# The square of two feed-forward pairs in three goes to PSUM instead of SBUF beside stage two

## The chip, the core and the metric

The kernel runs on one core of one Trainium2 chip. The metric is device time in microseconds (us) of one execution. Five engines work side by side, each through its own queue in order: TensorE (PE, with its weight loads shown as PEld), VectorE (DVE), ScalarE (ACT), GpSimd (POOL) and SyncE (SP), which here only issues DMAs. TensorE writes PSUM, eight banks of 512 float32 columns by 128 partitions; the other data lie in SBUF.

## The reference

```python
u = x * v                                   # 4 x 12480 x 128
h_filt = (np.maximum(pos_emb @ w1, 0.0) @ w2) * window
Uf = np.fft.rfft(u, n=2 * S, axis=1)
Hf = np.fft.rfft(h_filt, n=2 * S, axis=0)
y = np.fft.irfft(Uf * Hf[None], n=2 * S, axis=1)[:, :S]
z = (x * y).reshape(49920, 128)
out = (np.maximum(z @ w_in, 0.0) ** 2) @ w_out   # 128 -> 2048 -> 128
```

A long convolution by FFT for four batches, and after it a feed-forward whose activation is the squared relu. All of it is float32.

## The kernel before

The convolution of a batch goes through four stages (`stage1` to `stage4`), each a generator that yields 1, 2, 3 in every step; `chain()` strings the stages of all batches together. The feed-forward is cut into 98 token tiles of up to 512 tokens (`NM`) and, in each, into 8 pairs of 128 hidden rows (`NS`): 784 pairs. The main loop runs pair after pair and lets the convolution of the next batches advance in between with `adv(1)`, `adv(2)`, `adv(3)`. The schedule is manual: each engine runs its instructions in the order in which the code writes them. When all of the convolution is done, the rest of the pairs runs alone.

To keep float32 accuracy each operand is split into a high and a low part, and each product takes three matmuls (`mm3`, L100 to L102: high x high, low x high or its mirror, high x low). One pair goes as follows.

- `m_h` (L786): six matmuls write the pair's hidden values into a two-bank PSUM tile `A`. The pool `psa` has two such tiles, so four of the eight banks. One bank is `O`, three are the tiles `F` of the convolution.
- `m_g` (L792): ScalarE writes `r` = relu(`A`) to SBUF (L800), and then `gh`, the rounded high part of `r` squared (L803). The exact square comes in one of three ways. Way "p": VectorE writes max(`A`, 0) times `r` back over `A` (L805). Way "t": ScalarE squares `r` in place (L807). Way "b" also squares `r` in place, and VectorE makes `gh` from it (L814).
- `m_l` (L810): VectorE subtracts, `gl` = square minus `gh` (L819).
- `m_o` (L824): six matmuls, two pairs later in the loop, add the pair into `O`; the third of the six is the first that reads `gl`.

`way(n)` (L860) picks the way: beside stage two of a batch every third pair is "p" and the other two are "t"; beside stage three "b"; beside the other stages "p"; after the convolution "b".

In a turn of the loop the order on TensorE is: `m_h` of pair n, `m_o` of pair n-2, then the convolution's matmuls. Beside stage two these are L386, which write an `F` bank. VectorE multiplies that by the filter's spectrum `ht` (L421, twice per step), ahead of the subtraction of the pair, and GpSimd combines the products (L423, L424). The spectrum is loaded by SyncE's queue one step ahead (`ht<-Hd`). While batch 1 is in the convolution, the loop also takes an extra stage-two step every few pairs (`EXTRA`); beside the stage two of batches 2 and 3 it does not. These three stretches of the run are called the first, second and third block below.

A tile of a pool can be given out again when the last instruction that uses it has run; the next `m_h` into it then waits for that instruction.

Of the kernel before, what the change touches and what calls it, by code (L numbers as in the profile page):

```python
# [11 lines left out]
AF = mybir.ActivationFunctionType  # L12
# [37 lines left out]
def hyena_moe_kernel(  # L50
# [19 lines left out]
    nc = tc.nc  # L70
# [721 lines left out]
    def m_g(A, p, n, between, way):  # L792

        r = p.tile([128, 2, GM], F32, tag="r", name="r")[:, :, :n]
        hi = p.tile([128, 2, GM], F32R, tag="gh", name="gh")[:, :, :n]
        h = A[:, :, :n]
        nc.scalar.activation(r, h, AF.Relu)  # L800
        between()
        if way != "b":
            nc.scalar.activation(hi, r, AF.Square)  # L803
        if way == "p":
            nc.vector.scalar_tensor_tensor(out=h, in0=h, scalar=0.0, in1=r, op0=ALU.max, op1=ALU.mult)  # L805
            return p, h, hi, way
        nc.scalar.activation(r, r, AF.Square)  # L807
        return p, r, hi, way

    def m_l(st, share):  # L810
        p, g, hi, way = st
# [60 lines left out]
    for i in range(NM):  # L872
        for f in range(NS):
            adv(1)
            A = m_h(zT, f)
            last = m_o(*pend.pop(0)) if len(pend) > 1 else None
            adv(2)
            if not nxt[0] and not tail:
                tail.append(ctx.enter_context(pool("tp")))
                tail[0].tile([128, TP], F32, name="shift", bufs=1)  # L880
            late.append((i, f, m_g(A, tail[0] if tail and f % 2 else mp, GN[i], lambda: m_out(last), way(i * NS + f))))
            while len(late) > len(tail):
                x, y, st = late.pop(0)
                pend.append((x, y, m_l(st, False)))
            if i + 1 < NM:
                if f == (1 if i else 3):
                    ready(i + 1)
                    zi = zload(i + 1)
                if f == (4 if i else 6):
                    nzT = zsplit(zi)  # L890
            adv(3)
            n = i * NS + f
            if stage[0] != since[0]:
                since = stage[0], n + 4
            owed += EXTRA[done[1] > 0]
            if owed >= 1 and stage[0] in (("s3", "s4") if done[1] else ("s2", "s3", "s4")) and nxt[0] == 1 and n >= since[1]:
                owed -= 1
                since = stage[0], n + 3
                for k in range(1, 4):
                    adv(k)  # L900
# [144 lines left out]
```

## Time and profile before

| | before |
|---|---|
| median of 3 runs | 3066.09 us (3065.58 to 3071.74) |
| the profiled execution | 3062.8 us |
| its span on the core | 3060.9 us |
| TensorE busy | 3021.9 us, 99% of the span |
| VectorE busy | 2510.9 us, 82% |
| ScalarE busy | 2389.7 us, 78% |
| GpSimd busy | 1469.1 us, 48% |
| granted TensorE clock | 0.999 |

The profile is one execution. Busy time is the time in which an engine runs an instruction; waits lie between. Matmuls are pipelined, so a matmul of 0.39 us may be followed by the next one 0.23 us later: for TensorE the starts tell more than the durations. "gl<-r,gh" reads: writes gl, reads r and gh. "<-DVE gl" behind a row names what ended the idle time ahead of it.

### The profile page before, as it was taken

To read this page: it belongs to the slowest core of one execution; us is meant where nothing else is said; L and a number is where in the kernel's file an instruction comes from. 1 tells how busy PE (TensorE), PEld (TensorE's weight loads), DVE (VectorE), ACT (ScalarE), POOL (GpSimd) and SP (SyncE) were. 2 spreads that over 40 slices of the span, in tenths; PEclk is the share of its full clock that TensorE was granted. 3 is DMA by queue.
4 is the path that set the end of the run, shared out by engine and by line. 5 is a ranking of instruction groups with operands and counts; after the bars stand their busy time and mean duration, and the time that the engine had idled before them with its cause. 6 is when DMAs were issued, how large, how long until landed. Compare 5 with 4: busy or idle time off the path is not lost.

```text
span 3060.9 us, 48765 instructions
## 1 busy us (share of the span) xinstructions
PE 3021.9 (99%) x16010; PEld 2557.2 (84%) x16010; DVE 2510.9 (82%) x3056; ACT 2389.7 (78%) x3110; POOL 1469.1 (48%) x1595
## 2 busy tenths in 40 slices
PE   9989999999999999999999999999999999999999
PEld 8768888878888888888888888888888888888887
DVE  7888888878878988878877898878877898777776
ACT  5557777777888787788888877788888877888887
POOL 1249665647544665556544665646544563000000
PEclk9999999999999999999999999999999999999999
DMA  5782665444101664334200575434300474000000
GB/s 181 275 291 75 158 170 139 120 116 148 44 22 47 166 169 124 117 109 125 80 15 27 139 179 145 131 93 120 104 22 15 111 177 109 25 24 26 24 26 20
DMA packets 288753, 322.00 MB, mean 105 GB/s; under 512 B 95716, under 2 KB 214484, under 8 KB 288500
## 3 DMA queue, kind: packets, MB, share of 16 engines
q1 hardware_dynamic: 259348, 268.40, 30.3%
q0 software_dynamic: 29152, 50.48, 6.3%
q8 instruction: 128, 2.10, 0.3%
q14 instruction: 125, 1.02, 0.1%
HBM read 230.35 MB, written 64.55 MB: 96 GB/s over the span
## 4 chain that ended last, share of the span: by engine, by line
PE 88%; DMA 3%; DVE 3%; POOL 2%; issue 2%; ACT 1%; SPq 1%; DVEq 0%; ACTq 0%; POOLq 0%
PE A L100 11%; PE A L101 11%; PE A L102 11%; PE O L102 8%; PE O L101 8%; PE O L100 8%; PE F L386 5%; PE F L498 5%; PE F L298 4%; PE F L100 4%; PE F L102 4%; PE F L101 4%; PE A L296 2%; POOL W L411 1%; DMA xt<-x 1%
## 5 line engine op out<-in xcount | busy, mean ns | idle before, releaser
L800 ACT ACTIVATE r<-A 128x1020 f32<-128x1020 f32 (+2 forms) x784 | 804.2, 1026 | 410.7 <-PE A L102 397.1
L819 DVE TENSOR_TENSOR gl<-r,gh 128x1020 fp32r<-128x1020 f32 (+1 forms) x434 | 637.3, 1468 | 105.1 <-ACT r L807 68.1
L100 PE MATMUL A<-zh,wt 128*128 128x510 f32 (+2 forms) x1568 | 667.3, 426 | 1.8 <-DVE gl L819 1.5
L101 PE MATMUL A<-zh,wt 128*128 128x510 f32 (+2 forms) x1568 | 610.2, 389 | 0.0
L102 PE MATMUL A<-zl,wt 128*128 128x510 f32 (+2 forms) x1568 | 609.9, 389 | 0.0
L803 ACT ACTIVATE gh<-r 128x1020 fp32r<-128x1020 f32 (+1 forms) x452 | 477.3, 1056 | 61.0 <-PE O L101 53.3
L102 PE MATMUL O<-gl,wt 128*128 128x510 f32 (+1 forms) x1216 | 475.8, 391 | 3.6 <-DVE gl L819 3.5
L805 DVE SCALAR_TENSOR_TENSOR A<-A,r 128x1020 f32<-128x1020 f32 (+1 forms) x349 | 424.3, 1216 | 64.9 <-ACT r L800 63.0
L819 DVE TENSOR_TENSOR gl<-A,gh 128x1020 fp32r<-128x1020 f32 (+1 forms) x349 | 425.2, 1218 | 63.5 <-ACT gh L803 20.3
L101 PE MATMUL O<-gh,wt 128*128 128x510 f32 (+1 forms) x1216 | 472.1, 388 | 0.0
L100 PE MATMUL O<-gh,wt 128*128 128x510 f32 (+1 forms) x1216 | 472.0, 388 | 0.0
L807 ACT ACTIVATE r<-r 128x1020 f32<-128x1020 f32 (+1 forms) x435 | 461.0, 1060 | 12.5
L814 DVE CAST gh<-r 128x1020 fp32r<-128x1020 f32 (+1 forms) x332 | 232.6, 701 | 211.7 <-ACT r L807 210.7
L783 POOL TENSOR_TENSOR zl<-zi,zh 128x510 fp32r<-128x510 f32 (+1 forms) x97 | 126.6, 1305 | 536.1 <-PE A L102 427.7
L571 POOL TENSOR_TENSOR al<-W,ah 104x512 fp32r<-104x512 f32 x214 | 282.2, 1319 | 187.8 <-ACT ah L565 185.8
L102 PEld LDWEIGHTS A<-zl,wt 128*128 128x128 f32 x1568 | 294.4, 188 | 63.1
L507 POOL TENSOR_TENSOR W<-c 104x224 f32<-104x224 f32 x256 | 215.5, 854 | 264.6 <-ACT c L505 261.5
L100 PEld LDWEIGHTS A<-zh,wt 128*128 128x128 f32 x1568 | 296.0, 189 | 51.2 <-DVE gl L819 4.7
L101 PEld LDWEIGHTS A<-zh,wt 128*128 128x128 f32 x1568 | 296.3, 189 | 42.7
L423 POOL TENSOR_TENSOR W<-W,m 112x256 f32<-112x256 f32 x156 | 167.9, 1076 | 229.0 <-DVE m L421 207.0
L102 PEld LDWEIGHTS O<-gl,wt 128*128 128x128 f32 x1216 | 228.0, 187 | 53.0 <-DVE gl L819 5.7
L101 PEld LDWEIGHTS O<-gh,wt 128*128 128x128 f32 x1216 | 227.8, 187 | 47.5
(126 smaller groups left out, 5413.2 us busy)
## 6 DMA issues: line engine op xcount, KB each, us to landing
ht<-Hd SPq DMA_DIRECT2D x208, 256.0 KB
tb<-t POOLq DMA_DIRECT2D x224, 208.0 KB, 3.5
xt<-x SPq DMA_DIRECT2D x224, 128.0 KB
xt<-xs SPq DMA_DIRECT2D x96, 224.0 KB
vt<-vs SPq DMA_DIRECT2D x96, 224.0 KB
zd<-zs SPq DMA_DIRECT2D x333, 64.0 KB
out<-ot SPq DMA_DIRECT2D x79, 255.0 KB
tb<-t2s SPq DMA_DIRECT2D x156, 112.0 KB
```

The costliest lines, as they stand in the source:

```text
L100: nc.tensor.matmul(o, lh, rh, start=first, stop=False)
L101: nc.tensor.matmul(o, ll, rh, start=False, stop=False)
L102: nc.tensor.matmul(o, lh, rl, start=False, stop=last)
L423: nc.gpsimd.tensor_sub(out=re[0], in0=re[0], in1=im[1])
L507: nc.gpsimd.tensor_sub(out=dst[:, 1], in0=c[:, :, 0:3:2], in1=c[:, :, 3:0:-2])
L571: eng.tensor_sub(out=lo, in0=w, in1=hi.bitcast(F32))
L800: nc.scalar.activation(r, h, AF.Relu)
L803: nc.scalar.activation(hi, r, AF.Square)
L805: nc.vector.scalar_tensor_tensor(out=h, in0=h, scalar=0.0, in1=r, op0=ALU.max, op1=ALU.mult)
L807: nc.scalar.activation(r, r, AF.Square)
L814: nc.vector.tensor_copy(hi, g)
L819: nc.vector.tensor_sub(out=lo, in0=g, in1=hi.bitcast(F32))
```

## The change

Where the way is "t", ScalarE's second square is written over the pair's PSUM tile `A` instead of over `r`. The subtraction of that pair (L819 before, L820 after, as all lines from there on move by one) then reads `A` and `gh` instead of `r` and `gh`. Ways "p" and "b" stay as they are.

```diff
@@ m_g
         if way == "p":
             nc.vector.scalar_tensor_tensor(out=h, in0=h, scalar=0.0, in1=r, op0=ALU.max, op1=ALU.mult)
             return p, h, hi, way
-        nc.scalar.activation(r, r, AF.Square)
-        return p, r, hi, way
+        g = h if way == "t" else r
+        nc.scalar.activation(g, r, AF.Square)
+        return p, g, hi, way
```

No engine's order changes; what changes is who waits for whom. On TensorE, at the start of the first block: the last matmuls of one pair's `m_o` and the first of the `m_h` of pair 6767 (a "t" pair, as is the pair 6713 that had the same PSUM tile). The number behind a name tells the tile apart.

```order
 L100 MATMUL O_6520<-gh_6707,wt_1568 128x510 [waits Activation_49]
 L101 MATMUL O_6520<-gh_6707,wt_1568 128x510
-L102 MATMUL O_6520<-gl_6711,wt_1568 128x510 [waits DVE_49]
+L102 MATMUL O_6520<-gl_6711,wt_1568 128x510
 L100 MATMUL O_6520<-gh_6707,wt_1568 128x510
 L101 MATMUL O_6520<-gh_6707,wt_1568 128x510
 L102 MATMUL O_6520<-gl_6711,wt_1568 128x510
-L100 MATMUL A_6767<-zh_6606,wt_1037 128x510 [waits Activation_49]
+L100 MATMUL A_6767<-zh_6606,wt_1037 128x510 [waits DVE_49]
 L101 MATMUL A_6767<-zh_6606,wt_1037 128x510
 L102 MATMUL A_6767<-zl_6607,wt_1037 128x510
```

The first matmul of `m_h` waited for ScalarE, which had read the tile with its relu; now it waits for VectorE, whose subtraction is the tile's last reader. The wait for VectorE at the third matmul of `m_o` is gone, since the earlier one covers it. In the built program before, the "t" pairs of a block all follow each other in one of the two tiles of `psa`, and the "p" pairs have the other to themselves, because a "t" tile comes free first; in the changed program the pairs alternate between the two, so each `m_h` waits for the subtraction of the pair two before it.

On ScalarE, the same pairs: relu, high part and square of two "t" pairs, and the start of a "p" pair.

```order
 L800 ACTIVATE r_6706<-A_6693 128x2x510 [waits DVE_49,PE_49]
 L803 ACTIVATE gh_6707<-r_6706 128x2x510 [waits DVE_49,PE_49,Activation_49]
-L807 ACTIVATE r_6706<-r_6706 128x2x510 [waits Activation_49]
+L808 ACTIVATE A_6693<-r_6706 128x2x510
 L800 ACTIVATE r_6726<-A_6713 128x2x510 [waits DVE_49,PE_49]
 L803 ACTIVATE gh_6727<-r_6726 128x2x510 [waits DVE_49,PE_49,Activation_49]
-L807 ACTIVATE r_6726<-r_6726 128x2x510 [waits Activation_49]
```

The square in place had to wait until the instruction that makes `gh` had read `r`; the square into `A` has no wait of its own.

## Rows read from the trace of the kernel before

**Rows 1.** The page: each engine's busy time; the chain that ended last.

```profile
PE 3021.9 (99%) x16010; PEld 2557.2 (84%) x16010; DVE 2510.9 (82%) x3056; ACT 2389.7 (78%) x3110; POOL 1469.1 (48%) x1595
...
PE 88%; DMA 3%; DVE 3%; POOL 2%; issue 2%; ACT 1%; SPq 1%; DVEq 0%; ACTq 0%; POOLq 0%
```

**Rows 2.** Busy us by stretch (PE, PEld, DVE, ACT, POOL): first two blocks.

```profile
635.00:787.00 152.00, 148.91 (x661) 121.10 (x659) 126.72 (x155) 110.03 (x111) 109.60 (x108) 1.00 0.48 139
1318.00:1503.00 185.00, 185.00 (x823) 151.90 (x822) 153.90 (x171) 149.06 (x151) 115.85 (x108) 1.00 0.42 121
```

**Rows 3.** The page, costliest groups: busy us, mean ns of one | idle before.

```profile
L807 ACT ACTIVATE r<-r 128x1020 f32<-128x1020 f32 (+1 forms) x435 | 461.0, 1060 | 12.5
L814 DVE CAST gh<-r 128x1020 fp32r<-128x1020 f32 (+1 forms) x332 | 232.6, 701 | 211.7 <-ACT r L807 210.7
```

**Rows 4.** Groups by shape, same columns: both subtractions, and a PSUM copy.

```profile
L819 DVE TENSOR_TENSOR gl<-r,gh 128x1020 fp32r<-128x1020 f32 x291 | 446.7, 1535 | 90.2 <-ACT r L807 68.1 <-PE A L102 1.9 <-PE F L498 0.5
L819 DVE TENSOR_TENSOR gl<-A,gh 128x1020 fp32r<-128x1020 f32 x341 | 416.5, 1221 | 62.5 <-ACT gh L803 20.3 <-ACT ah L565 1.0 <-PE A L102 0.6
...
L434 ACT COPY A<-F 112x256 f32<-112x256 f32 x52 | 18.1, 349 | 1.6
```

**Rows 5.** Timeline (start us, us, engine): VectorE and GpSimd around 2098.

```profile
2098.35 3.85 DVE L819 TENSOR_TENSOR gl<-r,gh 128x1020 fp32r<-128x1020 f32 x1 [0.42 <-ACT r L807]
...
2099.85 1.27 POOL L783 TENSOR_TENSOR zl<-zi,zh 128x510 fp32r<-128x510 f32 x1
```

**Rows 6.** Who waited for whom, first block: us in total, times, longest.

```profile
DVE W L421 <- DMA ht<-Hd: 13.2, 11, 3.7
...
PE O L102 <- DVE gl L819: 3.0, 2, 1.9
```

**Rows 7.** The same view, second block.

```profile
DVE W L421 <- DMA ht<-Hd: 5.1, 4, 1.8
```

**Rows 8.** The same view, third block.

```profile
DVE W L421 <- DMA ht<-Hd: 6.9, 7, 1.4
```

**Rows 9.** Timeline, first block: a late spectrum, its "p" pair, and TensorE.

```profile
698.41 0.69 DVE L421 TENSOR_TENSOR W<-F,ht 112x512 f32<-112x512 f32 x1 [1.15 <-DMA ht<-Hd]
...
702.16 1.22 DVE L819 TENSOR_TENSOR gl<-A,gh 128x1020 fp32r<-128x1020 f32 x1
702.17 0.59 PE L100 MATMUL A<-zh,wt 128*128 128x510 f32 x1
...
704.19 0.39 PE L102 MATMUL O<-gl,wt 128*128 128x510 f32 x1
```

**Rows 10.** Timeline, third block: a "p" pair with no late spectrum.

```profile
2069.74 1.22 DVE L819 TENSOR_TENSOR gl<-A,gh 128x1020 fp32r<-128x1020 f32 x1
...
2071.60 0.59 PE L100 MATMUL A<-zh,wt 128*128 128x510 f32 x1
```

**Rows 11.** Timeline: the first "t" pair of the first block.

```profile
622.74 1.22 DVE L819 TENSOR_TENSOR gl<-r,gh 128x1020 fp32r<-128x1020 f32 x1 [2.77 <-ACT r L807]
...
623.26 0.39 PE L100 MATMUL A<-zh,wt 128*128 128x510 f32 x1
```

**Rows 12.** Timeline: the end of the first block.

```profile
787.22 0.39 PE L100 MATMUL A<-zh,wt 128*128 128x510 f32 x1
...
787.34 1.27 DVE L819 TENSOR_TENSOR gl<-r,gh 128x1020 fp32r<-128x1020 f32 x1 [0.81 <-ACT r L807]
```

**Rows 13.** Timeline: the end of the third block.

```profile
2210.58 0.42 PE L100 MATMUL A<-zh,wt 128*128 128x510 f32 x1
...
2211.42 1.22 DVE L819 TENSOR_TENSOR gl<-A,gh 128x1020 fp32r<-128x1020 f32 x1
...
2212.70 0.50 PE L102 MATMUL O<-gl,wt 128*128 128x510 f32 x1
```

**Rows 14.** Timeline, ScalarE: a square and the instruction behind it.

```profile
2039.61 1.06 ACT L807 ACTIVATE r<-r 128x1020 f32<-128x1020 f32 x1
...
2040.57 0.60 ACT L782 CAST zh<-zi 128x510 fp32r<-128x510 f32 x1
```

## The prediction, made before the run

> **What bounds the kernel now.** I read the busy times and the chain that ended last first: TensorE is busy for 3021.9 of 3060.9 us and makes up 88% of the chain [rows 1]. The reader is to see that a gain on another engine is worth nothing here unless TensorE waited for it, while a wait put on TensorE is lost one for one. Next the stretches in which the change acts. In the second block TensorE is busy for 185.00 of 185.00 us, while VectorE has 153.90 and ScalarE 149.06; the first block has 148.91 of 152.00 [rows 2]; the third block's row reads as the second's. The clock was granted in full, 1.00, in both. Then the waits inside the blocks, and at last the timeline, to see how long before each `m_h` the subtraction of the pair two earlier had ended: that is the wait which the change adds.
>
> **The change part by part.** How many pairs: 435 squares in place, of which 332 belong to way "b" (each has a cast on VectorE), so 435 - 332 = 103 are of way "t" [rows 3]. They lie in the three blocks, some 34 in each.
>
> *The square itself.* The trace has no ScalarE write into PSUM of this size. Bounds: 0.70 us, what VectorE's cast of as many columns takes [rows 3], and 4 x 0.349 = 1.40 us, four copies of 256 columns into PSUM with their fixed part counted four times [rows 4]. I take 1.06 us, the square in place, the nearest row [rows 3]: no change. At 1.40 every "t" subtraction would come 0.34 us later, which ScalarE has room for, but which adds to the waits below. In place, the square waits for the instruction before it to end; an instruction without such a wait starts 2040.57 - 2039.61 = 0.96 us after a square of 1.06 us [rows 14]. So the "t" chain gets 0.1 us shorter.
>
> The trace has no two equal ScalarE instructions that differ in the destination alone. The Trainium skill, "ScalarE: Activation LUTs", section "Step-by-step: what each stage is for", calls PSUM the destination of lower latency for ScalarE, with the caveat that this is of use only if TensorE doesn't need most of PSUM. By the tip alone the sum would be a few tenths of a microsecond better; by its caveat it turns over, since this kernel's pools fill all eight banks. The rest of this part is what the caveat means here, from rows.
>
> *The subtraction.* Read from `r` it takes 1.535 us in the mean, read from `A` 1.221 us [rows 4]: 0.31 us x 103 = 32 us of VectorE's time go. They are not on TensorE's path: in the first block TensorE waited for `gl` twice, 3.0 us in all [rows 6], and in the second hardly at all [rows 2]. I cost them at nothing, except where they bring a subtraction forward (below).
>
> *The added wait.* Before, a "t" pair's tile was free after its relu. Now it is free after its subtraction, and `m_h` of pair n waits for that of pair n-2. The same subtraction was already needed by the third matmul of `m_o`, so it is needed earlier: by 704.19 - 702.17 = 2.02 us [rows 9]. "P" pairs had that tile to themselves and were late without harm: in rows 9 the subtraction ends at 702.16 + 1.22 = 703.38, while the `m_h` that will now wait for it started at 702.17. Queued behind the waiting `m_h` on TensorE are its other five matmuls, `m_o` of the pair two earlier and the convolution's L386; ScalarE's relu and VectorE's L421 wait for these. So TensorE's delay moves everything behind it. Where is `m_h` late, and how much?
>
> 1. First pairs of each block. No L386 is between them yet. The subtraction ends at 622.74 + 1.22 = 623.96, `m_h` started at 623.26 [rows 11]: 0.7 us late. Three blocks, and I add 0.4 us once for a second late pair in the first: 2.5 us.
> 2. Inside the first block. With the extra steps VectorE has two steps' L421 ahead of the "p" pair, so that pair has no time to spare, and what a late spectrum costs passes through. VectorE waited 13.2 us for spectra there, and 3.0 us of it already reached TensorE [rows 6]: 13.2 - 3.0 = 10.2 us. The example: a spectrum 1.15 us late gives an `m_h` that is 703.38 - 702.17 = 1.2 us late [rows 9].
> 3. Inside the other two. A "p" pair there has spare time: 2071.60 - (2069.74 + 1.22) = 0.64 us [rows 10]. VectorE waited 5.1 us in 4 waits [rows 7] and 6.9 us in 7 [rows 8]; less 0.64 us each, 12.0 - 11 x 0.64 = 5.0 us. A few fall on a "t" pair and cost less.
> 4. Ends of the blocks. The L421 of the last step and the change of way find TensorE without L386 to fill in. 787.34 + 1.27 - 787.22 = 1.4 us late in the first [rows 12], 2211.42 + 1.22 - 2210.58 = 2.1 us in the third, of which the third matmul of `m_o`, 2212.70 - 2210.58 = 2.12 us behind, has already waited for some 0.1 us more than the 2.02 us of rows 9 [rows 13]. With a follower that is late as well I take 2 us each: 6.0 us.
>
> Sum: 2.5 + 10.2 + 5.0 + 6.0 = 23.7 us. About 27 late places, each 0.1 us less late through the earlier square: -2.7 us. Net +21 us. Against the profiled execution, 3062.8 us, that is 3084 us; the median of the runs before is 3.3 us above it, so I predict 3087 us.
>
> The bounds of this sum: if a held TensorE gives the spectra time to arrive, terms 2 and 3 vanish and 2.5 + 6.0 - 0.6 = 8 us stay; if nothing is absorbed, the chain is not shortened and the square takes 1.40 us, some 27 x 0.44 = 12 us come on top, 33 us. So 3074 to 3099 us for this case.
>
> **The rivals.**
> - *Faster subtraction wins.* A subtraction from SBUF can be held up by GpSimd: the one at 2098.35 took 3.85 us and ended about when it could after GpSimd's L783 at 2099.85 + 1.27 = 2101.12 [rows 5]. The one from `A` takes 1.22 us, so VectorE runs ahead, subtractions come up to 2.6 us earlier, and the new waits find them done. TensorE then only saves the 3.0 us that it waited in the first block [rows 6]: 3063 us. It decides if VectorE's backlog is what makes "p" pairs late; that needs the gain to exceed the 0.7 to 2.1 us of rows 9 and 11 to 13. For it: 32 us less work. Against it: in those rows the late pair comes after an idle VectorE, which waited for a spectrum or for ScalarE, so there was no backlog to shorten. The Trainium skill, "SBUF — State Buffer", section "SBUF: two separate sides", describes the pair of ports that VectorE and GpSimd share as an exclusive lock, which a VectorE operation with two SBUF inputs takes part in; by that rule the lock goes with `r`, and rows 5 agree.
> - *The delays mostly heal.* A delay of TensorE lets late spectra catch up, and only terms 1 and 4 remain: +8 us, or half of that if they heal in part as well, 3070 to 3074 us. For it: the spectra's loads are issued ahead. Against it: the load waits for a buffer that VectorE frees, which follows TensorE, so it is delayed as well.
> - *Delays breed more.* Each `m_h` that waits delays the relu, and with three ScalarE instructions and a subtraction between two waits the loop `m_h` to `m_h` closes on itself in most turns: another 0.2 us in each of 103 "t" pairs, 3087 + 20 = 3107 us. Against it: "p" pairs had 0.64 us to spare [rows 10].
>
> **How the numbers follow.** The forecast gets 0.70; healing 0.13; faster subtraction 0.10; breeding 0.07. The range 3068 to 3104 us holds the forecast with its own bounds, healing, and a part of breeding. A measurement of this kernel can tell about 0.2%, 6 us, from no change. Slower by more than that (above 3072 us): the forecast, breeding, and about half of healing, 0.83. Within 0.2%: the other half of healing and most of the faster subtraction, 0.14. Faster by more: 0.03, since TensorE waits too little for 6 us to be had.
>
> **What would show it.** Right: rows for TensorE waiting at L100 with `A` for VectorE's subtraction (now L820), some 30 of them, 0.3 to 3 us each, most behind a "p" pair after a late spectrum and at the ends of the blocks; subtractions of one duration, 1.22 us; the wait at `m_o` gone; the blocks longer by 3 to 14 us each, the first the most; everything outside the blocks as long as before. Wrong: blocks of the old length (healing or the faster subtraction), or a wait at nearly every L100 with `A` (breeding), or a square into PSUM far from 1.06 us.

## The result, and the profile after

The changed kernel takes 3085.03 us (median of 4 runs, 3079.27 to 3086.43); before it was 3065.84 us (4 runs, 3063.84 to 3071.74). The ratio is 1.0057, 95% interval 1.0045 to 1.0068: 19 us slower. Predicted were 3087 us and slower.

The page after has, against [rows 1], shorter busy times on three engines and a longer span:

```profile
span 3084.2 us, 48715 instructions
PE 3030.0 (98%) x16010; PEld 2560.3 (83%) x16010; DVE 2484.0 (81%) x3056; ACT 2377.0 (77%) x3110; POOL 1404.6 (46%) x1595
...
L820 DVE TENSOR_TENSOR gl<-A,gh 128x1020 fp32r<-128x1020 f32 (+1 forms) x452 | 550.8, 1219 | 170.5 <-ACT A L808 103.7
L100 PE MATMUL A<-zh,wt 128*128 128x510 f32 (+2 forms) x1568 | 668.0, 426 | 17.0 <-DVE gl L820 16.3
```

VectorE is busy for 27 us less, ScalarE for 13 us less, GpSimd for 65 us less. The last goes with the 103 subtractions: in hold_inplace below, which subtracts from `r` again, GpSimd is back at 1472.6 us. TensorE now waits at L100 for `gl`, 16.3 us in all (1.5 us before); VectorE's subtraction from `A` takes 1.22 us as in [rows 4]. The new instruction has a row of its own among the groups by shape, here with the two squares of the same kernel that are written to SBUF, one in place and one into another tile:

```profile
L803 ACT ACTIVATE gh<-r 128x1020 fp32r<-128x1020 f32 x444 | 469.7, 1058 | 60.4 <-PE O L101 51.3 <-DVE W L310 1.9 <-DVE z L612 1.2
...
L808 ACT ACTIVATE r<-r 128x1020 f32<-128x1020 f32 x188 | 199.0, 1058 | 5.2
...
L808 ACT ACTIVATE A<-r 128x1020 f32<-128x1020 f32 x103 | 103.9, 1009 | 0.0
```

103 squares, as counted, and 1.009 us each where the square into SBUF takes 1.058 us, in place or not. So the write into PSUM is the cheaper one.

The waits of TensorE for `gl` over the whole kernel after (us in total, times, longest):

```profile
PEld A L100 <- DVE gl L820: 26.0, 27, 4.6
...
PE A L100 <- DVE gl L820: 16.3, 17, 4.2
```

The first row is the weight load, which may wait beside running matmuls; the second is the matmul itself. Before, the same two rows had 4.7 us in 10 waits and 1.5 us in 4. In the first block alone, against [rows 6]:

```profile
PEld A L100 <- DVE gl L820: 12.6, 6, 4.6
DVE W L421 <- DMA ht<-Hd: 10.8, 7, 4.3
PE A L100 <- DVE gl L820: 10.1, 5, 4.2
```

The same view of the second block, and of the third:

```profile
PE A L100 <- DVE gl L820: 2.5, 3, 0.9
```

```profile
PE A L100 <- DVE gl L820: 1.0, 2, 0.8
```

The wait at `m_o` (L102) of [rows 6] is gone, and five waits of 10.1 us have come at `m_h`. The longest, in the timeline after:

```profile
669.30 1.03 PE L386 MATMUL F<-W,tb 120*112 120x256 f32 x4
670.66 0.69 DVE L421 TENSOR_TENSOR W<-F,ht 112x512 f32<-112x512 f32 x1 [4.32 <-DMA ht<-Hd]
...
673.22 1.22 DVE L820 TENSOR_TENSOR gl<-A,gh 128x1020 fp32r<-128x1020 f32 x1
674.49 0.79 PE L100 MATMUL A<-zh,wt 128*128 128x510 f32 x1 [4.16 <-DVE gl L820]
675.08 0.63 PE L101 MATMUL A<-zh,wt 128*128 128x510 f32 x1
675.50 0.63 PE L102 MATMUL A<-zl,wt 128*128 128x510 f32 x1
```

The reader is to see two things. VectorE waits 4.32 us for a spectrum, its queue stands still, and the subtraction of a "p" pair ends at 674.44; TensorE, idle for 4.16 us, starts right behind. And from there its matmuls follow each other by 675.50 - 675.08 = 0.42 us, where it was 0.23 us. The stretches of the kernel after, with the granted clock third from the end of a row:

```profile
674.00:680.00 6.00, 5.51 (x14) 4.39 (x15) 3.95 (x6) 1.41 (x2) 3.32 (x5) 0.54 0.22 66
775.00:782.00 7.00, 6.24 (x15) 4.86 (x16) 4.22 (x6) 2.13 (x3) 3.30 (x4) 0.51 0.23 73
646.00:651.00 5.00, 4.27 (x19) 3.54 (x20) 4.20 (x6) 3.05 (x4) 3.55 (x4) 1.00 0.34 98
```

The waits ahead of the third and the second of these stretches, from the timeline of the same kernel:

```profile
646.73 0.50 PE L100 MATMUL A<-zh,wt 128*128 128x510 f32 x1 [1.08 <-DVE gl L820]
...
775.76 0.79 PE L100 MATMUL A<-zh,wt 128*128 128x510 f32 x1 [3.00 <-DVE gl L820]
```

After 4.16 and 3.00 us of waiting TensorE was granted half of its clock, 1.2 in place of 2.4 GHz; after 1.08 us it kept the whole.

**Where the time went.** The start of the first matmul of `m_h` of one and the same pair, compared between the two traces, tells what has been lost up to there. In the kernel before, pairs 82 and 120, which enclose the inner part of the first block:

```profile
625.98 0.39 PE L100 MATMUL A<-zh,wt 128*128 128x510 f32 x1
...
777.95 0.59 PE L100 MATMUL A<-zh,wt 128*128 128x510 f32 x1
```

and in the kernel after:

```profile
630.11 0.50 PE L100 MATMUL A<-zh,wt 128*128 128x510 f32 x1
...
794.66 0.59 PE L100 MATMUL A<-zh,wt 128*128 128x510 f32 x1
```

4.1 us behind at the one, 16.7 us at the other: the inner part lost 12.6 us. Done for all parts, for this kernel and those of the experiments, against the one profiled execution before (us; negative is gained):

| kernel | block 1: first pairs, inside, end | block 2 | block 3 | between and behind the blocks | ratio of times (95%) |
|---|---|---|---|---|---|
| the change | 0.8, 12.6, 1.0 | 0.7, 2.1, 0.3 | 0.5, 1.6, 0.3 | 0.2 | 1.0057 (1.0045 to 1.0068) |
| hold_only | 1.4, 11.6, 1.5 | 1.1, 3.9, 0.7 | 1.1, 6.3, 0.4 | 27.9 | 1.0187 (1.0173 to 1.0200) |
| hold_inplace | 1.3, 9.8, 1.2 | 1.0, 2.6, 0.4 | 1.1, 2.1, 0.2 | 0.4 | 1.0059 (1.0046 to 1.0071) |
| hold_early | 1.3, -2.6, 1.2 | 1.0, 1.5, 0.4 | 1.1, 0.6, -0.5 | 0.2 | 1.0008 (1.0000 to 1.0017) |
| late_blocks | 0.0, 0.0, 0.0 | 0.7, 1.5, 0.9 | 0.7, 1.2, 0.0 | -0.2 | 1.0011 (1.0002 to 1.0020) |
| early_after | 0.8, -4.0, 1.0 | 0.7, 0.0, -0.2 | 0.5, 0.0, -0.4 | -0.3 | 0.9993 (0.9985 to 1.0002) |
| early_before | 0.0, -3.8, 0.0 | 0.0, 0.0, -0.2 | 0.0, 0.0, -0.4 | -0.2 | 0.9989 (0.9980 to 0.9998) |
| subfirst_after | 0.8, 0.2, 1.4 | 0.7, 0.0, 0.2 | 0.5, 0.0, 0.6 | 0.3 | 1.0011 (1.0002 to 1.0019) |
| shift_only | 0.3, 2.4, 0.4 | 0.2, 1.7, 0.0 | 0.1, 1.7, 0.4 | 25.5 | 1.0104 (1.0089 to 1.0120) |

(Block 1 is pairs 76 to 130 with cuts at 82 and 120, block 2 pairs 261 to 325 with cuts at 265 and 316, block 3 pairs 451 to 516 with cuts at 456 and 507. What lies ahead of pair 76 differs by -1.5 to 6.0 us from execution to execution, also where nothing was changed in it, and is left out.) For the change the parts come to some 20 us; the medians differ by 19.2 us.

### The profile page after: what moved, and what is told of

Same layout as the page of the kernel before. It is cut to its first block, busy times and chain, and to the rows that moved or that the text cites. A ratio compares the mean times of both kernels' runs of the same rounds, so it can differ in the third digit from the quotient of the medians.

```text
span 3084.2 us, 48715 instructions
## 1 busy us (share of the span) xinstructions
PE 3030.0 (98%) x16010; PEld 2560.3 (83%) x16010; DVE 2484.0 (81%) x3056; ACT 2377.0 (77%) x3110; POOL 1404.6 (46%) x1595
## 4 chain that ended last, share of the span: by engine, by line
PE 88%; DVE 3%; DMA 3%; POOL 2%; issue 2%; ACT 1%; SPq 1%; DVEq 0%; ACTq 0%; POOLq 0%
PE A L100 11%; PE A L101 11%; PE A L102 11%; PE O L102 8%; PE O L100 8%; PE O L101 8%; PE F L498 5%; PE F L386 5%; PE F L298 4%; PE F L100 4%; PE F L102 4%; PE F L101 4%; PE A L296 2%; DMA ht<-Hd 1%; POOL W L411 1%
## 5 line engine op out<-in xcount | busy, mean ns | idle before, releaser
L820 DVE TENSOR_TENSOR gl<-A,gh 128x1020 fp32r<-128x1020 f32 (+1 forms) x452 | 550.8, 1219 | 170.5 <-ACT A L808 103.7
L100 PE MATMUL A<-zh,wt 128*128 128x510 f32 (+2 forms) x1568 | 668.0, 426 | 17.0 <-DVE gl L820 16.3
L102 PE MATMUL A<-zl,wt 128*128 128x510 f32 (+2 forms) x1568 | 610.6, 389 | 0.0
L820 DVE TENSOR_TENSOR gl<-r,gh 128x1020 fp32r<-128x1020 f32 (+1 forms) x331 | 483.8, 1461 | 35.0 <-PE F L498 0.5
L102 PE MATMUL O<-gl,wt 128*128 128x510 f32 (+1 forms) x1216 | 475.9, 391 | 0.3 <-DVE gl L820 0.3
L100 PE MATMUL O<-gh,wt 128*128 128x510 f32 (+1 forms) x1216 | 472.6, 389 | 0.0
L808 ACT ACTIVATE r<-r 128x1020 f32<-128x1020 f32 (+1 forms) x332 | 351.8, 1060 | 9.3
L100 PEld LDWEIGHTS A<-zh,wt 128*128 128x128 f32 x1568 | 296.3, 189 | 72.4 <-DVE gl L820 26.0
L102 PEld LDWEIGHTS A<-zl,wt 128*128 128x128 f32 x1568 | 294.8, 188 | 63.6
L423 POOL TENSOR_TENSOR W<-W,m 112x256 f32<-112x256 f32 x156 | 133.7, 857 | 305.2 <-DVE m L421 226.4
L102 PEld LDWEIGHTS O<-gl,wt 128*128 128x128 f32 x1216 | 228.4, 188 | 48.3 <-DVE gl L820 0.7
L100 PEld LDWEIGHTS O<-gh,wt 128*128 128x128 f32 x1216 | 228.5, 188 | 47.7
```

The costliest lines, as they stand in the source:

```text
L100: nc.tensor.matmul(o, lh, rh, start=first, stop=False)
L102: nc.tensor.matmul(o, lh, rl, start=False, stop=last)
L808: nc.scalar.activation(g, r, AF.Square)
L820: nc.vector.tensor_sub(out=lo, in0=g, in1=hi.bitcast(F32))
```

## The experiments

Theory: a "t" pair's PSUM tile, held until the subtraction, makes `m_h` wait for it; late spectra make that wait long. Rivals: ScalarE's writes into PSUM cost by themselves; each pair costs the same, because the loop from one `m_h` to the next is too long anyway; the spectra cost by themselves.

**hold_only: the tile held, the squares in SBUF.** The squares stay in `r`; a one-column read of `A` behind the subtraction of "t" pairs holds the tile.

```diff
+    held_a = mp.tile([128, 1], F32, name="held_a", bufs=1)
...
             nc.vector.tensor_sub(out=lo, in0=g, in1=hi.bitcast(F32))
+        if way == "t":
+            nc.vector.tensor_copy(held_a, h[:, 1, :1])
```

> The squares stay in SBUF as before; only a one-column VectorE copy behind each 't' subtraction reads A, so that the PSUM tile is held until then. Theory (the held tile makes m_h wait for the subtraction): as slow as the change or a little slower, 3080 to 3095 us, with TensorE waiting for VectorE at L100 with A in the same places (12 us or more in the first block), since the subtractions also stay at 1.5 us. Rival (ScalarE's writes into PSUM cost, by standing in the way of TensorE's writes): no such write here, so the time before, 3064 to 3069 us.

Measured: 3120.44 us (ratio 1.0187), far over both. The blocks lost 28 us, but another 28 us went outside them, where the kernel does what it did before. Each matmul of `m_h` was slower (mean in ns behind the comma), first in the kernel before and then in this one:

```profile
L101 PE MATMUL A<-zh,wt 128*128 128x510 f32 x1264 | 492.2, 389 | 0.0
```

```profile
L101 PE MATMUL A<-zh,wt 128*128 128x510 f32 x1264 | 499.6, 395 | 0.0
```

In the built program the added tile had moved `zh` and `zl` in SBUF by 32 bytes. As a test of holding alone it is spoilt, so it was made again without the tile.

**hold_inplace: the same without a new tile.** The one column of `A` is copied onto itself.

```diff
...
             nc.vector.tensor_sub(out=lo, in0=g, in1=hi.bitcast(F32))
+        if way == "t":
+            nc.vector.tensor_copy(h[:, 1, :1], h[:, 1, :1])
```

> As hold_only, but the one-column copy goes from A to A, so that no SBUF tile is added: in hold_only the added tile moved the tiles zh and zl by 32 bytes, and all matmuls that read them ran 6 ns slower, outside the blocks too. Theory (held tile): the blocks lose what they lost in hold_only, 14.6, 5.7 and 7.8 us, and nothing else does: 3088 to 3096 us. Rival (ScalarE's writes into PSUM): 3064 to 3068 us.

Measured: 3085.33 us (5 runs, 3076.00 to 3088.19), before on the same chip 3065.30 us. Ratio 1.0059, with the change at 1.0057. I had expected 3 us more, from the blocks of hold_only, which its slower matmuls had made dearer. TensorE's waits in the first block of this kernel:

```profile
PEld A L100 <- DVE gl L819: 13.1, 8, 3.8
DVE W L421 <- DMA ht<-Hd: 11.2, 7, 3.0
PE A L100 <- DVE gl L819: 10.0, 6, 3.4
```

10.0 us at L100 for `gl`, with the change 10.1. ScalarE writes no square into PSUM here, and TensorE waits as long at the same place: the held tile is the cause, and the writes as such cost nothing that could be seen. That the two totals agree so closely is in part chance. Blocks 2 and 3 lose 7.4 us here and 5.5 us with the change; this kernel still has the slower subtraction from `r`, and the added copy. The first block loses 12.3 us here and 14.4 us with the change, while the clock stood at half for a shorter time: 0.72 and 0.76 in the stretches that answer to those with 0.54 and 0.51. The copy, and these stretches:

```profile
L821 DVE COPY A<-A 128x1 f32<-128x1 f32 x103 | 16.0, 155 | 0.1
```

```profile
674.00:680.00 6.00, 5.40 (x17) 4.30 (x18) 4.13 (x7) 2.17 (x3) 4.23 (x5) 0.72 0.22 71
774.50:781.50 7.00, 6.27 (x22) 5.11 (x23) 4.26 (x7) 3.09 (x4) 4.12 (x4) 0.76 0.22 69
```

**shift_only: what a moved tile costs.** The kernel before with an unused tile of one column.

```diff
+    pad = mp.tile([128, 1], F32, name="pad", bufs=1)
+    nc.vector.memset(pad, 0.0)
```

> The kernel before with one unused 1-column SBUF tile, which moves zh and zl by 32 bytes and nothing else. If their place is what slowed the matmuls in hold_only: 3088 to 3096 us, evenly spread over all pairs. If hold_only was slow for another reason: 3062 to 3068 us.

Measured: 3097.97 us, ratio 1.0104, 2 us over the range and spread over all pairs (25.5 us of it outside the blocks). The row of this kernel that answers to the ones above:

```profile
L101 PE MATMUL A<-zh,wt 128*128 128x510 f32 x1264 | 498.4, 394 | 0.0
```

So it was the place of `zh` and `zl` that slowed hold_only outside the blocks. Why one place is slower than the other 32 bytes on, no run here tells, nor why the matmuls of `m_o`, whose operands did not move, went from 389 to 391 ns.

**late_blocks: the change for batches 2 and 3 only.**

```diff
-        g = h if way == "t" else r
+        g = h if way == "t" and done[1] else r
```

> The change only for batches 2 and 3 (second and third block); the first block as before. Theory (late spectra, which the first block has because of its extra steps, carry most of the loss): the first block costs nothing, the other two what they cost in the change, 3 and 2 us: 3069 to 3073 us. Rival (each of the 103 pairs costs the same, 19 us / 103): two thirds of the loss stay, 3077 to 3081 us.

Measured: 3067.67 us, 1 us under the range; before on the same chip 3064.63 us; ratio 1.0011 (1.0002 to 1.0020). The first block costs nothing now, the other two 3.1 and 1.9 us. Two thirds of the pairs carry about a quarter of the loss; the rival "each pair the same" falls.

**early_after and early_before: the spectrum one step earlier.** In the change, and in the kernel before.

```diff
-            lh = 4 if big else 0
+            lh = 4 if big else 1
...
-                ht = p.tile([128, D, 2, 2], F32, tag="ht", name="ht", bufs=5 if big else 2)
+                ht = p.tile([128, D, 2, 2], F32, tag="ht", name="ht", bufs=5 if big else 3)
```

> The change, with the spectrum ht loaded one step earlier into a third buffer, so that it is there when VectorE asks for it. Theory: the long waits at m_h behind late spectra go, and with them the two stretches at half clock in the first block; the first pairs and the ends of the blocks stay, and 'p' pairs with no spare time in the first block: 3066 to 3073 us. Rival (the loop from m_h through relu, squares and subtraction to the next m_h is too long by itself, whatever the spectra): 3080 us or more.

> The kernel before with the spectrum one step earlier. Control for the run beside it: theory, only the 3.0 us go that TensorE waited for gl at m_o in the first block, 3060 to 3065 us. If this gains as much as the change does from the same edit, 10 us or more, the spectra cost by themselves and not through the held tile.

Measured: 3062.82 us for the change with early spectra, 3060.96 us for the kernel before with them, against 3064.63 us before. The first is 3 us under its range: inside the first block it came out 4.0 us ahead of the kernel before, and the "p" pairs with no spare time, which I had expected to keep a loss, kept none. With the change the edit gains 12.6 + 4.0 = 16.6 us inside the first block, without it 3.8 us: the late spectra cost 3.8 us by themselves and the other 12.8 us through the held tile. What TensorE still waits for in the first block of early_after:

```profile
DVE W L421 <- DMA ht<-Hd: 1.1, 2, 0.6
PEld A L100 <- DVE gl L820: 0.9, 4, 0.4
```

VectorE waits 1.1 us for spectra where it was 10.8, and TensorE no longer waits at `m_h` in this stretch, only a weight load does, 0.9 us in all. Inside blocks 2 and 3 nothing is left at all (0.0 and 0.0). Why a spectrum was late is to be read in SyncE's queue of the kernel before, for the latest one of that kernel:

```profile
657.08 0.34 SPq L839 DMA_DIRECT2D out<-ot  x1
657.48 2.98 SPq L774 DMA_DIRECT2D zi<-zd  x5
660.55 0.41 SPq L372 DMA_DIRECT2D tb<-t2s  x1
661.07 0.38 SPq L378 DMA_DIRECT2D ht<-Hd  x1
```

and in VectorE's, which frees the buffer for this load with the first of these and waits for the spectrum ahead of the second:

```profile
656.62 0.68 DVE L421 TENSOR_TENSOR m<-F,ht 112x512 f32<-112x512 f32 x1
...
665.25 0.69 DVE L421 TENSOR_TENSOR W<-F,ht 112x512 f32<-112x512 f32 x1 [3.70 <-DMA ht<-Hd]
```

Every eighth pair an output and up to five loads of tokens are issued; here they took SyncE from 657.08 to 660.46, so the load went out 3.8 us after its buffer was free at 656.62 + 0.68 = 657.30, and VectorE waited 3.70 us. The other late spectra were not traced back one by one. The kernel before with early spectra is the fastest of all that ran, and is under 1 by its interval, by 0.1%.

**hold_early: hold_inplace with early spectra.** Both edits above.

> hold_inplace with the spectrum one step earlier. Theory (late spectra are what makes the held tile dear): the bodies of the blocks lose nothing, as in early_after, 3063 to 3068 us. Rival (the subtraction from r, which GpSimd can hold up, is late often enough by itself, and the change is spared that by its faster subtraction): the second and third block keep 3 to 7 us each, 3070 to 3080 us.

Measured: 3067.36 us, ratio 1.0008 (1.0000 to 1.0017). The first block's inside gains 2.6 us, blocks 2 and 3 keep 1.5 and 0.6 us inside, against 0.0 and 0.0 in early_after. So the late spectra carry nearly all, as the theory had it. The rest, some 2 us in blocks 2 and 3 and 1.4 us inside the first, goes to the slower subtraction from `r` or to the added copy of 0.155 us behind it; no run separates the two. The rival may have a part of the truth, at less than its size.

**subfirst_after: the subtraction ahead of the products.** Beside stage two `adv(2)` stands behind `m_l`.

```diff
-            adv(2)
+            s2 = stage[0] == "s2"
+            if not s2:
+                adv(2)
...
                 pend.append((x, y, m_l(st, False)))
+            if s2:
+                adv(2)
```

> The change, with a pair's instructions on VectorE ahead of the stage-two products of the same turn (adv(2) behind m_l beside stage two). A late spectrum then stands ahead of the next pair, whose relu comes a pair later. Theory: most late spectra have landed by then, 3062 to 3070 us. Rival (what matters is that VectorE's queue holds two products per step anywhere ahead of a subtraction): 3080 us or more.

Measured: 3069.06 us, ratio 1.0011 (1.0002 to 1.0019). Another cure for the same thing: the spectrum isn't loaded sooner, VectorE asks for it later. Inside the blocks 0.2, 0.0 and 0.0 us are lost. The number of products in the queue is the same as in the change, so it was the wait among them.

## Why the prediction was right, point by point

- **The added wait** came where it was looked for: all five waits of the matmul inside the first block are behind a "p" pair, pairs 84, 90, 99, 108 and 114, and behind a late spectrum. (For pair 114 the profile puts VectorE's wait, shown below, down to a matmul that ended at the same moment; in the kernel before, VectorE waits 2.87 us for a spectrum at this place.) I had expected some 30 places; the weight load waited at 27 and the matmul itself at 17 in the whole kernel (10 and 4 before the change).
- **First pairs** (2.5 us): 0.8 + 0.7 + 0.5 = 2.0 us.
- **Inside the first block** (10.2 us): 12.6 us. VectorE waited 13.9 us for spectra, the 10.8 us of the row above and these 3.1 us:

```profile
771.93 0.69 DVE L421 TENSOR_TENSOR W<-F,ht 112x512 f32<-112x512 f32 x1 [3.15 <-PE O L102]
```

Not all of it passed through, as I had it: waits at `m_h` rose to 10.1 us, and 3.0 us at `m_o` went, which makes 7.1 us, less than the 10.2 us. Most of the rest is the clock: after the two longest waits some 12 matmuls each came every 0.42 us in place of 0.23 us, 2 x 12 x 0.2 = 4.8 us. Nothing in the prediction had that. The term was mis-sized both ways, and the two errors nearly cancel.
- **Inside the other two** (5.0 us): 2.1 + 1.6 = 3.7 us.
- **Ends** (6.0 us): 1.0 + 0.3 + 0.3 = 1.6 us, the worst of the terms. At the places of rows 12 and 13 `m_h` does not need the subtraction of the pair two before it, as the text ahead of the prediction says of each `m_h`. The block has just ended there: the pair before is already of way "b", its tile is free after its relu, and in the built program the next `m_h` takes that one. The place of rows 13 in the kernel after:

```profile
2233.64 0.41 PE L100 MATMUL A<-zh,wt 128*128 128x510 f32 x1
...
2234.70 1.22 DVE L820 TENSOR_TENSOR gl<-A,gh 128x1020 fp32r<-128x1020 f32 x1
```

`m_h` started without a wait, 2.3 us before the subtraction ended that it was to wait for. At the place of rows 12 it waited 0.54 us, for the relu. At the end of the second block it waited 0.87 us for a "p" pair's subtraction, and a wait of 0.55 us at `m_o` went.
- **The sum** (21 us): 2.0 + 12.6 + 3.7 + 1.6 = 19.9 us in the blocks, 0.2 us outside. The mechanism and the places were right; that the sum came so close is in part luck. It had 2.4 us too little inside the first block, against 0.5, 1.3 and 4.4 us too much for first pairs, the other two blocks and the ends, and 2.7 us taken off for the shorter chain.
- **The square** taken at 1.06 us came to 1.009 us, and the shorter chain (-2.7 us) is not to be told apart in these runs. Here the trace agrees with the tip of the Trainium skill, "ScalarE: Activation LUTs", section "Step-by-step: what each stage is for", that PSUM is ScalarE's quicker destination, by 0.05 us; and with its caveat, by 19 us.
- **The faster subtraction** came as read from the rows, 1.22 us, and freed 27 us of VectorE. It did not pay for the held tile: hold_inplace, without it, is as slow as the change, and what it is worth once the tile is held is at most the 0.15% between hold_early and early_after.
- **Breeding** did not happen: with early spectra the loop closes with no wait inside the blocks.

## What to carry to other kernels

Where an engine writes its result decides for how long the buffer under it is taken; if the engine that sets the pace needs that buffer next, an intermediate that is cheaper to write and cheaper to read can still lose. Before moving one, list for each use of the buffer when its last reader ends and when its next writer starts, and look at what stands ahead of that reader in its queue: here transfers late by a few microseconds cost 3.8 us in all, until the next matmul had to wait behind them. Two remedies worked here, and neither is at the instruction that shows the wait: one step of prefetch for the late transfer, or letting the wait for that transfer stand behind the urgent reader instead of ahead of it.

## What the runs showed of the hardware

- TensorE idle for 4.16 us, and again for 3.00 us, was granted half of its clock, 1.2 GHz, for the next 5 to 6 us (0.54 and 0.51 in the stretches above); after 1.08 us it kept the whole. Each of the two stalls cost some 2.4 us more than itself.
- `zh` and `zl` moved by 32 bytes in SBUF slowed each matmul that reads them from 389 to 394 ns in the mean, and the whole kernel by 1.0% (shift_only). A tile of four bytes per partition in the wrong place cost more than the change under study. What an experiment adds to SBUF has to leave the addresses of the rest where they were.
- A ScalarE square of 1020 columns takes 1.009 us into PSUM and 1.058 us into SBUF, from the same SBUF source.
- Subtracting from `A` in PSUM in place of `r` in SBUF took 103 VectorE subtractions to 1.22 us each, and GpSimd was busy for 1404.6 us in place of 1469.1 us beside them.
